# A two-layer linear-attention and Mish kernel: the last query tile's subtraction half a block sooner, low parts used later, the first block reordered

## The chip, the cores and the metric

The kernel runs on one core of a Trainium2 chip. The metric is the device time of one execution in microseconds (us); of several runs the median counts. A core has five engines with a queue of instructions each: TensorE (PE, matrix products, with weight loads listed as PEld), VectorE (DVE), ScalarE (ACT), GpSimd (POOL) and SyncE (SP, which issues the transfers from and to memory). An engine runs its own instructions in order and waits at semaphores for those of others.

## The reference

The input x has 2048 rows of 640 values; there are 32 heads of 20 values. Two layers, with the same weights, follow one another; each adds to x first the attention and then a dense part:

```python
qkv = x @ wqkv                                  # x is layer-normed
pq, pk = q @ w_phi, k @ w_phi                   # per head, 20 x 20
phi_q = concatenate([softmax(pq), softmax(-pq)])  # 40 features per head
phi_k = concatenate([softmax(pk), softmax(-pk)])
kv, z = phi_k^T v, sum over rows of phi_k
o = (phi_q kv) / (phi_q z + 1e-6)
x = x + o @ wo
h = layernorm(x) @ w1 + b1                      # 640 -> 1536
x = x + (h * tanh(softplus(h))) @ w2            # Mish
```

All of it is fp32. The two inner softmaxes need the maximum and the minimum of each head's 20 values.

## The kernel before, in words

**Precision.** A TensorE product of fp32 accuracy is made of three: each operand is split into a high part, rounded to the engine's fast fp32 format (names ending in `h`), and a low part, the remainder (`l`). A product is high x high, high x low weight, low x high weight, one matmul each; `project_half` (L399) issues these three for each of the five slices of 128 of the inner dimension. A high part is a copy by ACT, a low part a subtraction by DVE or POOL.

**Tiles and stages.** The 2048 rows are 8 blocks of 256, each of two tiles of 128. For each layer `attend_first` goes over the blocks and makes values, key features with the running sum `kv`, and query features, which go to memory; `attend_second` goes over them again: average by `kv`, divide, multiply by `wo`, add to x, and take the statistics of the next layer norm; `dense` is the Mish part.

**Folding.** w_phi is multiplied into the weights of q and k once, at the start of layer 0, so that a projection gives pq or pk (less its head's reference column) at once. `fold` (L263) is a matmul of a slice of the loaded weights (`raw`) with differences of w_phi (`big`, made by DVE at L256). A slice k of the first half (304 columns) is t = 0, 1, 2, of the second half t = 3, 4, 5, in one of five PSUM banks. `fold_parts` then makes the high part by an ACT copy (L272) and the low part by a DVE subtraction (L274): `r2h`, `r2l` for queries, `r1h`, `r1l` for keys and values.

**The first block.** For layer 0 the first block is written out by hand (L525 to L655), and for all five engines the order of the code is the order of the instructions. It holds warm-up transposes (L531, `TURNS` of them), the loads, statistics and normalization of the block's two rows of tiles, the folds, `FirstRows.turn` (L345, five transposes of a normalized tile) and `split` (high parts `xth` by ACT, low parts `xtl` by DVE, L355), the query projections of the two halves, both query tiles' features, the key folds, and the values. The value weights are not folded; `v_weights` splits them with ACT (L139) and POOL (L140) from staging tiles that SP's queue fills.

**Features** (L427): copy to SBUF by ACT (L436), maximum and minimum by DVE (L441), subtraction of the maximum (L444, by POOL for queries and DVE for keys), subtraction from the minimum (L446, DVE), exponential (ACT), sum and reciprocal (DVE, L452, L453), multiplication (POOL, L454). It is a generator: each `next` or `tail` advances it by one step.

**The second pass.** `block(b)` of `attend_second` issues for its two tiles `Rows.half(0)` and `half(1)`: 15 matmuls with `wo`, addition to x (L805) and statistics (L806). Between them stand the next block's average and the transposes of its rows (L317), their low parts `xtl` (L323), and steps of the last two query tiles' features: `tail(0)` and `tail(1)`, as many as the code says. The order of PE, SP and DVE is that of the code here. POOL also makes the low parts of the weights of the dense part (L161). The order of everything that is not said to be written out is set by the framework's list scheduler.

Of the kernel before, what the change touches and what calls it, by code (L numbers as in the profile page):

```python
# [10 lines left out]
AF = mybir.ActivationFunctionType  # L11
# [13 lines left out]
BT = 2  # L25
# [15 lines left out]
TURNS = 24  # L41
# [10 lines left out]
def kernel(  # L52
# [25 lines left out]
    def one_tile():  # L78
        return psum.tile([P, 512], F32, tag="one", name="one", bufs=4)
# [42 lines left out]
    def act(*args, **kw):  # L122

        if last_act[0] is None or written[0]:
            ins = nc.scalar.activation(*args, **kw)  # L125
        else:
            with tc.issue_after(last_act[0]):
                ins = nc.scalar.activation(*args, **kw)
        last_act[0] = ins.ins
# [5 lines left out]
    def split(hi, lo, src, stage, low=nc.vector):  # L135

        st = stage()[:, :D]
        nc.sync.dma_start(st, src)
        nc.scalar.activation(hi, st, AF.Copy)  # L139
        low.tensor_tensor(lo, st, hi.bitcast(F32), op=ALU.subtract)  # L140
# [38 lines left out]
    def v_weights(ws, low=nc.vector):  # L179

        for k in V_ORDER:
            split(ws[k][0][:, D:2 * D], ws[k][1][:, D:2 * D], wv[k * P:(k + 1) * P, :],
                  (row_tile, row_tile, v_tile, v_tile, big_tile)[k], low)
            yield
# [175 lines left out]
    def normed(b, xt):  # L360

        xn = [row_tile() for _ in range(BT)]
        for t in range(BT):
            act(xn[t], xt[:, t, :], AF.Identity,
                                 bias=stats[:, b, 1, t:t + 1], scale=stats[:, b, 0, t:t + 1])
        return Transposed(xn)
# [32 lines left out]
    def project_half(ps, xts, t, ws, col, c, ks=range(KD), w=HC, final=KD - 1):  # L399
        sl = slice(t * P, (t + 1) * P)  # L400
        cs = slice(col + c * w, col + (c + 1) * w)
        for k in ks:
            h, l, wh, wl = xts.hs[k], xts.ls[k], ws[k][0][:, cs], ws[k][1][:, cs]
            for n, (a, r) in enumerate(((h, wh), (h, wl), (l, wh))):
                nc.tensor.matmul(ps[:, :w], a[:, sl], r, start=(k == 0 and n == 0),  # L405
                                 stop=(k == final and n == 2))
# [55 lines left out]
    def attend_first(layer, x_src, first):  # L462
# [62 lines left out]
        if first is None:  # L525
            E = mybir.EngineType
            with tc.manual_schedule(engines={E.PE, E.SP, E.Activation, E.DVE, E.Pool}):
# [14 lines left out]
                def banks_of_five():  # L542
                    ma, mb = mm_tile(), mm_tile()
                    return [ma[:, 0], ma[:, 1], mb[:, 0], mb[:, 1], one_tile()]
# [18 lines left out]
                q_ws = [r2_pair(k) for k in range(KD)]  # L563
                kv_ws = [r1_pair(k) for k in range(KD)]
                xts = FirstRows()
                banks = banks_of_five()
                for t in range(2):
                    for k in range(KD):
                        fold(banks[k], bd, raw, k, t)
                turned, last = one_tile(), one_tile()  # L570
                xts.turn(0, rows[0], turned, last[:, :P])
                for k in range(KD):
                    fold(banks[k], bd, raw, k, 2)
                xts.split(0)
                query_parts(banks, 0, (0, 1))
                query_parts(banks, 0, (2, 3))
                query_parts(banks, 0, (4,))
# [3 lines left out]
                project_half(pq[0], xts, 0, q_ws, 0, 0, w=FC)  # L581
                vw = v_weights(kv_ws, nc.gpsimd)
                for _ in range(3):
                    next(vw)
                banks = banks_of_five()
                for k in range(KD):
                    for t in range(3, 6):
                        fold(banks[k], bd, raw, k, t)
                query_parts(banks, 1, (0, 1))
                normalize_first(1)  # L590
                query_parts(banks, 1, (2, 3))
                query_parts(banks, 1, (4,))
                xts.turn(1, rows[1], one_tile(), last[:, P:2 * P])
                xts.split(1)
                pq.append(one_tile())
                project_half(pq[1], xts, 0, q_ws, 0, 1, w=FC)
                next(vw)
                next(vw)
                raw = load_raw(1)
                g0 = queries(xts, 0, pq)  # L600
                next(g0)
                next(g0)
                p1 = project(xts, 1, q_ws, 0, w=FC)
                next(g0)
                g1 = queries(xts, 1, p1)
                next(g1)

# [8 lines left out]
                parts[0](0)  # L616
                next(g1)
                parts[1](0)
                parts[0](1)
                next(g1)  # L620
                parts[1](1)
                parts[2](0)
                parts[3](0)
                next(g0)
                parts[2](1)
                parts[3](1)
                parts.append(fold_keys(4))
                parts[4](0)
                vs = [v_tile() for _ in range(BT)]
                xt = fetch(x_src, 1)  # L630
                mvs = [norm_stats(t, xt) for t in range(BT)]
                norm_scale(1, mvs)
                ready = last_scale[0]
                v = [values(xts, t, vs[t]) for t in range(BT)]
                next(v[0])
                next(g1)
                parts[4](1)
                nxt = normed(1, xt)
# [114 lines left out]
    def attend_second(x_src, x_dst, acc, fetches, makes, fetch_next, begin_next):  # L753
# [41 lines left out]
        class Rows:  # L795


            def __init__(self, b, t, cur):
                self.t, self.xt, self.cur = t, xs[b], cur
                self.bn = work.tile([P, 2, 6], F32, tag="bn", name="bn", bufs=2)  # L800

            def half(self, c, ps):
                project_half(ps, self.cur, self.t, o_ws, 0, c)
                part = self.xt[:, self.t, c * HC:(c + 1) * HC]
                nc.vector.tensor_tensor(part, ps[:, :HC], part, op=ALU.add)  # L805
                nc.vector.bn_stats(self.bn[:, c], part)  # L806
# [6 lines left out]
        def block(b, cur, behind=()):  # L813
# [38 lines left out]
            for _ in range((0, 2, 1, 2)[b] if b < 4 else 0):  # L852
                tail(1)
# [254 lines left out]
```

## Time and profile before

| | us |
|---|---|
| median of 3 runs | 1361.92 |
| lowest, highest run | 1361.70, 1361.93 |
| profiled execution, its own time | 1361.4 |
| its span | 1359.6 |
| PE busy | 1348.8 (99%) |
| DVE, ACT, POOL busy | 1067.7, 585.1, 473.6 |

A row of the timeline has start, duration, engine, line, operation, output from inputs, and shape, and in brackets the idle time before it with what ended it. Matmuls overlap: a matmul's duration is longer than the step from one to the next, so that steps are read from start to start. In a list of waits stand total, count and mean.

### The profile page before, as it was taken

Reading aid. Unit: us, or ns where it says so; the run is one execution under the profiler, and the core shown is the slowest. Engines: PE = TensorE matmul, PEld = TensorE weight load, DVE = VectorE, ACT = ScalarE, POOL = GpSimd, SP = SyncE. Lnnn points to the kernel's source line nnn. Section 1 sums busy time; section 2 is a strip of 40 time slices with the busy share of each in tenths; the row PEclk is TensorE's granted clock in tenths of the full one; section 3 lists DMA queues with packets and bytes.
Section 4 is the critical chain, followed back from the end, with each engine's and each line's share of the span. In section 5 each row is a group of like instructions: output and inputs, shape, how many; then the busy total and the mean of one; then the engine's idle time right before and its main releaser. Section 6 shows DMA issues by size and latency. Waiting matters only on the chain.

```text
span 1359.6 us, 30929 instructions
## 1 busy us (share of the span) xinstructions
PE 1348.8 (99%) x12890; PEld 1335.9 (98%) x12890; DVE 1067.7 (79%) x1805; ACT 585.1 (43%) x1039; POOL 473.6 (35%) x361
## 2 busy tenths in 40 slices
PE   8999999999999999999999999999999999999998
PEld 8999999999999999999999999999999999999998
DVE  5988788887787887778778988888768776676775
ACT  5443444222454545445444344432236444444443
POOL 3345544434222222222226556743441211111111
PEclk9999999999999999999999999999999999999999
DMA  9614335798614442334473534468964231233200
GB/s 345 174 42 78 80 60 125 186 281 280 194 39 98 117 117 69 61 104 104 143 236 60 120 74 78 80 164 242 278 235 126 78 87 23 86 97 98 73 25 20
DMA packets 350613, 169.21 MB, mean 124 GB/s; under 512 B 287225, under 2 KB 323817, under 8 KB 350473
## 3 DMA queue, kind: packets, MB, share of 16 engines
q1 hardware_dynamic: 350473, 167.23, 46.0%
q8 instruction: 101, 1.65, 0.5%
q14 instruction: 39, 0.32, 0.1%
HBM read 104.61 MB, written 62.59 MB: 123 GB/s over the span
## 4 chain that ended last, share of the span: by engine, by line
PE 96%; DVE 2%; DMA 1%; ACT 0%; issue 0%; POOL 0%; SPq 0%; DVEq 0%
PE mm L405 28%; PE mm L946 25%; PE one L904 25%; PE one L405 12%; PE mm L771 3%; PE one L317 2%; PE one L490 2%; DMA big<-in_wv 0%; DVE big L446 0%; DMA raw<-in_wqk_t 0%; DVE xt L805 0%; DVE bn L806 0%; DVE r L452 0%; ACT r L125 0%; POOL r L444 0%
## 5 line engine op out<-in xcount | busy, mean ns | idle before, releaser
L946 PE MATMUL mm<-r2h,ol 128*128 128x320 f32 x1280 | 304.9, 309 | 0.0
L930 POOL TENSOR_TENSOR ol<-big,ol 128x512 fp32r<-128x512 f32 (+1 forms) x98 | 131.0, 1337 | 484.0 <-ACT ol L929 384.2
L904 PE MATMUL one<-xtl,r1h 128*128 128x256 f32 x960 | 268.2, 279 | 0.0
L904 PE MATMUL one<-xth,r1l 128*128 128x256 f32 x960 | 268.0, 279 | 0.0
L904 PE MATMUL one<-xth,r1h 128*128 128x256 f32 x960 | 265.9, 279 | 0.0
L946 PEld LDWEIGHTS mm<-r2h,ol 128*128 128x128 f32 x1280 | 219.2, 188 | 0.0
L946 PE MATMUL mm<-r2l,ol 128*128 128x320 f32 x640 | 197.3, 309 | 0.0
L405 PE MATMUL mm<-r1h,xth 128*128 128x304 f32 (+1 forms) x600 | 184.9, 308 | 0.0
L405 PE MATMUL mm<-r1l,xth 128*128 128x304 f32 (+1 forms) x600 | 183.7, 306 | 0.0
L405 PE MATMUL mm<-r1h,xtl 128*128 128x304 f32 (+1 forms) x600 | 183.5, 306 | 0.0
L904 PEld LDWEIGHTS one<-xtl,r1h 128*128 128x128 f32 x960 | 180.4, 188 | 0.0
L904 PEld LDWEIGHTS one<-xth,r1l 128*128 128x128 f32 x960 | 180.4, 188 | 0.0
L904 PEld LDWEIGHTS one<-xth,r1h 128*128 128x128 f32 x960 | 179.6, 188 | 0.0
L919 DVE TENSOR_SCALAR big<-big 128x512 f32<-128x512 f32 (+1 forms) x98 | 55.9, 571 | 113.2 <-ACT big L917 110.8
L454 POOL TENSOR_TENSOR big<-big,r 128x1280 f32<-128x1280 f32 x42 | 101.0, 2410 | 67.0 <-DVE r L453 42.8
L917 ACT ACTIVATE big<-one,b1s 128x256 f32<-128x256 f32 x192 | 80.9, 468 | 93.7 <-PE one L904 92.9
L946 PEld LDWEIGHTS mm<-r2l,ol 128*128 128x128 f32 x640 | 120.2, 188 | 0.0
L921 ACT ACTIVATE big<-big,two 128x512 f32<-128x512 f32 (+1 forms) x98 | 70.1, 716 | 113.6 <-DVE big L920 113.5
L929 ACT ACTIVATE ol<-big 128x512 fp32r<-128x512 f32 (+1 forms) x98 | 60.9, 622 | 132.9 <-DVE big L928 132.8
L405 PE MATMUL one<-r2h,xth 128*128 128x320 f32 (+1 forms) x350 | 111.5, 318 | 2.9 <-DVE xt L805 1.9
L405 PEld LDWEIGHTS mm<-r1h,xth 128*128 128x128 f32 x600 | 112.8, 188 | 0.6
L405 PEld LDWEIGHTS mm<-r1h,xtl 128*128 128x128 f32 x600 | 112.7, 188 | 0.3
(169 smaller groups left out, 3123.3 us busy)
## 6 DMA issues: line engine op xcount, KB each, us to landing
big<-e_d SPq DMA_DIRECT2D x30, 640.0 KB, 6.0
x_d<-xt SPq DMA_DIRECT2D x23, 640.0 KB, 3.9
e_d<-r SPq DMA_DIRECT2D x88, 160.0 KB, 4.1
xt<-x_d SPq DMA_DIRECT2D x22, 640.0 KB, 5.7
n_d<-xn SPq DMA_DIRECT2D x176, 80.0 KB, 2.3
xt<-in_x SPq DMA_DIRECT2D x15, 640.0 KB, 4.5
xn<-x_d SPq DMA_DIRECT2D x28, 320.0 KB, 4.3
v<-n_d SPq DMA_DIRECT2D x30, 256.0 KB, 3.2
```

What stands on the lines that cost most here:

```text
L317: nc.tensor.transpose(ps[:, c, t * P:(t + 1) * P], self.rows[t][:, (c0 + c) * P:(c0 + c + 1) * P], ident)
L405: nc.tensor.matmul(ps[:, :w], a[:, sl], r, start=(k == 0 and n == 0), stop=(k == final and n == 2))
L454: nc.gpsimd.tensor_tensor(eg, eg, r.unsqueeze(2).to_broadcast([P, 2 * H, DH]), op=ALU.mult)
L490: nc.tensor.matmul(kva[32 * q:32 * q + DH + 1, c:c + 2 * DH], v[:, (DH + 1) * h:(DH + 1) * (h + 1)], e[:, 2 * DH * h:2 * DH * (h + 1)], st ...
L771: nc.tensor.matmul(po[c][64 * q:64 * q + 64, GW * j:GW * j + w], phs[g][:n, s0:s0 + 64], kvb[:n, g, :w], start=True, stop=True)
L904: nc.tensor.matmul(ph[:, j, :], l, r, start=(n == 0), stop=(n == 3 * KD - 1))
L917: exps[0] = nc.scalar.activation(part(ta, 0)[:, j - js.start], ph[:, j, :], AF.Exp, bias=b1s[:, 2 * pr + j:2 * pr + j + 1]).ins
L919: nc.vector.tensor_scalar_min(e, e, E_CAP)
L921: nc.scalar.activation(r, n, AF.Ln, bias=two)
L929: nc.scalar.activation(ah[:, js], n, AF.Copy)
L930: nc.gpsimd.tensor_tensor(al[:, js], n, ah[:, js].bitcast(F32), op=ALU.subtract)
L946: nc.tensor.matmul(pys[t][:, c, :HC], l[:, j, sl], r, start=(f == 0 and n == 0), stop=(f == KF - 1 and n == 2))
```

## The change

The change has ten parts.

1. The warm-up has 20 transposes instead of 24.
2. In SP's queue the last three slices of the first weights stand ahead of the first block's second tile; the value weights are all loaded together next, and the key weights sooner.
3. The first tile of rows is normalized in two halves, one by ACT and one by DVE.
4. The bank order of the folds starts with another bank, and the turn of the first tile stands ahead of the last three folds of t = 1 and those of t = 2. DVE makes the differences for t = 3 to 5 later.
5. Of each half of the query weights all high parts are made first, then all low ones; the projection takes the ten products with high weights first and the five with low ones behind them. In the first half the folds of the next bank stand between.
6. ACT's order: the first value weight's copy ahead and the others behind the second tile's normalization, and the second query tile's copy ahead of the first one's exponential.
7. `pool_sub` is given as `i >= BT`: for the first two query tiles of each layer both subtractions are DVE's.
8. In the first block, the next block's statistics and normalization, and the key weights' parts, stand sooner.
9. In the first half of block 0 of the second pass the products of two slices with low inputs stand behind the four others of both.
10. In block 1 of the second pass one `tail(1)` stands ahead of the second tile's first half instead of at the block's end.

On PE, in layer 0's first block, from the warm-up to the first projections (`raw` a slice of weights, `r2h` and `r2l` high and low folded query weights, `xth` and `xtl` high and low rows). Before:

```order
L263 MATMUL mm<-big,raw_146 128x114 x4
L263 MATMUL one<-big,raw_146 128x114
L345 MATMUL one<-ident,xn 128x128 x5
L263 MATMUL mm<-big,raw_148 128x114 x4
L263 MATMUL one<-big,raw_148 128x114
L405 MATMUL one<-r2h_176,xth 128x304
L405 MATMUL one<-r2l_177,xth 128x304
L405 MATMUL one<-r2h_176,xtl 128x304
L405 MATMUL one<-r2h_178,xth 128x304
L405 MATMUL one<-r2l_179,xth 128x304
L405 MATMUL one<-r2h_178,xtl 128x304
```

And now:

```order
L273 MATMUL mm<-big,raw_142 128x114
L355 MATMUL one<-ident,xn 128x128 x5
L273 MATMUL mm<-big,raw_142 128x114 x3
L273 MATMUL one<-big,raw_144 128x114
L273 MATMUL mm<-big,raw_144 128x114 x4
L417 MATMUL one<-r2h_156,xth 128x304
L417 MATMUL one<-r2h_156,xtl 128x304
L417 MATMUL one<-r2h_158,xth 128x304
L417 MATMUL one<-r2h_158,xtl 128x304
L417 MATMUL one<-r2h_160,xth 128x304
L417 MATMUL one<-r2h_160,xtl 128x304
```

The transposes stand eight folds ahead of the first projection instead of five, and low weights come into it ten matmuls later.

On DVE, in the second pass of layer 0, block 1 (`big` the last query tile, `xt` the rows with the residual, `xtl` low parts of the next block's). Before:

```order
L810 BN_AGGR mv<-bn 128x2
L295 TENSOR_SCALAR stats<-mv,stats 128x1 x2
L805 TENSOR_TENSOR xt<-one,xt 128x320
L806 BN_STATS bn<-xt 128x6
L323 TENSOR_TENSOR xtl<-one,xth 128x512 x2
L323 TENSOR_TENSOR xtl<-one,xth 128x256
L805 TENSOR_TENSOR xt<-one,xt 128x320
L806 BN_STATS bn<-xt 128x6
L810 BN_AGGR mv<-bn 128x2
L446 TENSOR_TENSOR big<-m,big 128x32x20
L786 TENSOR_SCALAR den<-mm 128x24
```

And now:

```order
L846 BN_AGGR mv<-bn 128x2
L305 TENSOR_SCALAR stats<-mv,stats 128x1 x2
L458 TENSOR_TENSOR big<-m,big 128x32x20
L841 TENSOR_TENSOR xt<-one,xt 128x320
L842 BN_STATS bn<-xt 128x6
L333 TENSOR_TENSOR xtl<-one,xth 128x512 x2
L333 TENSOR_TENSOR xtl<-one,xth 128x256
```

The subtraction stands ahead of the second tile's first addition and of three low parts, and no longer behind them.

On POOL, in layer 1's first pass, which the list scheduler orders (`xtl` low parts of rows, `r_...` and `big` query and key tiles). Before:

```order
L323 TENSOR_TENSOR xtl<-xn,xth 128x512 x2
L454 TENSOR_TENSOR big<-big,r 128x1280
L323 TENSOR_TENSOR xtl<-xn,xth 128x256
L444 TENSOR_TENSOR big<-big,m 128x32x20
L454 TENSOR_TENSOR big<-big,r 128x1280
```

And now:

```order
L333 TENSOR_TENSOR xtl<-xn,xth 128x512
L466 TENSOR_TENSOR big<-big,r 128x1280
L333 TENSOR_TENSOR xtl<-xn,xth 128x512
L466 TENSOR_TENSOR big<-big,r 128x1280
L333 TENSOR_TENSOR xtl<-xn,xth 128x256
L456 TENSOR_TENSOR big<-big,m 128x32x20
```

A multiplication has come between the two larger low parts, so that two stand ahead of the small one instead of one.

The diff, cut to its core:

```diff
-TURNS = 24
+TURNS = 20
...
-    def project_half(ps, xts, t, ws, col, c, ks=range(KD), w=HC, final=KD - 1):
+    def project_half(ps, xts, t, ws, col, c, ks=range(KD), w=HC, final=KD - 1, ns=(0, 1, 2), end=2):
...
-            for n, (a, r) in enumerate(((h, wh), (h, wl), (l, wh))):
+            for n in ns:
+                a, r = ((h, wh), (h, wl), (l, wh))[n]
...
-            yield from features(project(xts, i % BT, q_ws, 0, w=FC) if ps is None else ps, e, True, i >= NT - 2)
+            yield from features(project(xts, i % BT, q_ws, 0, w=FC) if ps is None else ps, e, i >= BT, i >= NT - 2)
...
+                raw += load_raw(0, range(3, 6))
                 fetch_first(1)
-                raw += load_raw(0, range(3, 6))
...
+                vw = v_weights(kv_ws, nc.gpsimd, ahead=True)
...
-                normalize_first(0)
+                act(rows[0][:, :HC], xt[:, 0, :HC], AF.Identity, bias=stats[:, 0, 1, :1], scale=stats[:, 0, 0, :1])
+                nc.vector.tensor_scalar(rows[0][:, HC:], xt[:, 0, HC:], stats[:, 0, 0, :1], stats[:, 0, 1, :1],
+                                        op0=ALU.mult, op1=ALU.add)
...
+                query_folds(0, range(KD))
+                query_folds(1, range(2))
+                turned, last = one_tile(), one_tile()
+                xts.turn(0, rows[0], turned, last[:, :P])
+                xts.split(0)
+                query_folds(1, range(2, KD))
+                query_folds(2, range(KD))
...
+                query_high(*range(KD))
+                query_low(*range(KD))
+                raw_k = load_raw(1)
...
+                project_half(pq[0], xts, 0, q_ws, 0, 0, w=FC, ns=(0, 2), end=None)
+                next(vw)
+                banks = banks_of_five()
+                for t in range(3, 6):
+                    fold(banks[0], bd, raw, 0, t)
+                query_parts(banks, 1, (0,))
+                project_half(pq[0], xts, 0, q_ws, 0, 0, w=FC, ns=(1,), end=1)
+                for k in range(1, KD):
+                    for t in range(3, 6):
+                        fold(banks[k], bd, raw, k, t)
+                normalize_first(1)
+                query_parts(banks, 1, (1, 2))
+                query_parts(banks, 1, (3, 4))
...
             def half(self, c, ps):
-                project_half(ps, self.cur, self.t, o_ws, 0, c)
+                if self.b == self.t == c == 0:
+                    for ks in ((0, 1), (2, 3), (4,)):
+                        for ns in ((0, 1), (2,)):
+                            project_half(ps, self.cur, 0, o_ws, 0, 0, ks, ns=ns)
+                else:
+                    project_half(ps, self.cur, self.t, o_ws, 0, c)
...
+            if b == 1:
+                tail(1)
             if b == NB - 2:
...
-            for _ in range((0, 2, 1, 2)[b] if b < 4 else 0):
+            for _ in range((0, 1, 1, 2)[b] if b < 4 else 0):
```

More of the change, by code (lines that the diff above doesn't have):

```diff
@@ L358, in row_tile, with normed_rows @@
         return work.tile([P, D], F32, tag="xn", name="xn", bufs=4)
+    def normed_rows(b, xt):
+        xn = [row_tile() for _ in range(BT)]
+        normalize(b, xn, [xt[:, t, :] for t in range(BT)])
+        return xn
     def normed(b, xt):
[L362 to L366, printed above, removed]
+        return Transposed(normed_rows(b, xt))
     def normalize(b, dst, src):
@@ L631, in attend_first @@
                 mvs = [norm_stats(t, xt) for t in range(BT)]
+                for k in range(2):
+                    for n in range(2):
+                        parts[k](n)
                 norm_scale(1, mvs)
                 ready = last_scale[0]
+                next(g1)
+                parts[2](0)
+                parts[3](0)
+                parts[2](1)
+                parts[3](1)
+                nxt_rows = normed_rows(1, xt)
+                next(g1)
+                next(g0)
+                parts.append(fold_keys(4))
+                parts[4](0)
+                parts[4](1)
                 v = [values(xts, t, vs[t]) for t in range(BT)]
```

96 lines of the change are left out of this document (39 added, 57 removed).

## The prediction

> **What bounds the kernel now.** I read the page's busy shares and chain first, then the waits of TensorE, then the windows, and last the timelines of the places where TensorE waits.
>
> ```profile
> span 1359.6 us, 30929 instructions
> PE 1348.8 (99%) x12890; PEld 1335.9 (98%) x12890; DVE 1067.7 (79%) x1805; ACT 585.1 (43%) x1039; POOL 473.6 (35%) x361
> PE 96%; DVE 2%; DMA 1%; ACT 0%; issue 0%; POOL 0%; SPq 0%; DVEq 0%
> ```
>
> TensorE (PE) is busy for 1348.8 of 1359.6 us and carries 96% of the chain that ended last. The matmuls are, in kind and number, the same after the change but for four warm-up transposes, so only time that PE loses between them can be won. The waits of PE, grouped (total, count, mean of one), and two windows (length; busy PE, weight loads, DVE, ACT, POOL; granted clock, DMA share, GB/s):
>
> ```profile
> PE one L405 <- DVE xt L805: 1.9, 2, 0.9
> PE one L405 <- DVE r2l L274: 1.4, 2, 1.0
> PE one L405 <- DVE xtl L323: 0.3, 2, 0.2
> 0.00:42.00 42.00, 38.48 (x281) 36.95 (x282) 25.23 (x61) 22.11 (x50) 15.90 (x21) 1.00 0.97 346
> 42.00:255.00 213.00, 213.00 (x2570) 210.23 (x2570) 179.68 (x259) 91.74 (x157) 101.91 (x65) 1.00 0.43 89
> ```
>
> Three groups hold 3.6 us: a residual addition that PE waits for once per layer, low weight parts at the start, and a low part at the start of each second pass. The first 42 us lack 3.5 us of PE work; the 213 us behind them lack none, and DVE, busy for 180 of those, still delays nobody. Idle times count the modelled end of the last matmul, so below I use start against start.
>
> **The change, part by part: the start.** PE there:
>
> ```profile
> 1.34 4.38 PE L531 MATMUL one<-ident 128*128 128x128 f32 x24 [1.34 <-POOL ident masks.py:199]
> 5.87 1.12 PE L263 MATMUL mm<-big,raw 120*128 120x114 f32 x8 [0.15 <-DMA raw<-in_wqk_t]
> 8.54 0.71 PE L345 MATMUL one<-ident,xn 128*128 128x128 f32 x5
> 10.41 0.40 PE L405 MATMUL one<-r2h,xth 128*128 128x304 f32 x1
> 11.31 0.41 PE L405 MATMUL one<-r2l,xth 128*128 128x304 f32 x1 [0.49 <-DVE r2l L274]
> 11.55 0.30 PE L405 MATMUL one<-r2h,xtl 128*128 128x304 f32 x1
> 11.69 0.30 PE L405 MATMUL one<-r2h,xth 128*128 128x304 f32 x1
> 17.00 0.76 PE L345 MATMUL one<-ident,xn 128*128 128x128 f32 x5
> 18.71 0.41 PE L405 MATMUL one<-r2h,xth 128*128 128x304 f32 x1 [0.95 <-DVE r2l L274]
> 30.82 1.31 PE L263 MATMUL mm<-big,raw 120*128 120x114 f32 x10 [0.23 <-DVE r1l L274]
> ```
>
> The first fold at 5.87 waits for its weights from memory, and their loads stay where they are in the queue; so the four warm-up transposes fewer gain nothing, and I cost them at zero, covered by that load. A matmul takes 0.14 (11.55 to 11.69). From 10.41 to 11.31 one matmul stands, so 0.76 is lost; from 17.00 to 18.71 stand five transposes (0.11 each, 0.55 in all), so 1.16 is lost; the wait at 30.82 is worth 0.2 to 0.4. The engines that feed these places:
>
> ```profile
> 14.94 0.21 DVE L295 TENSOR_SCALAR stats<-mv,stats 128x1 f32<-128x1 f32 x1 [0.96 <-POOL stats L291]
> 9.18 0.83 ACT L125 ACTIVATE xth<-one 128x256 fp32r<-128x256 f32 x3 [1.79 <-PE one L345]
> 9.88 1.52 ACT L272 ACTIVATE r2h<-mm 128x342 fp32r<-128x342 f32 x4
> 16.02 0.92 ACT L125 ACTIVATE xn<-xt,stats 128x640 f32<-128x640 f32 x1
> ```
>
> In the first half, the first turn goes ahead of eight folds: two on ACT and DVE at once instead of ACT alone (0.92 for a row) make the normalized row sooner, and the ten matmuls with high weights stand ahead of the five with low ones, with three folds of the next part between. So the wait at 11.31 (0.76) goes; ACT's five copies of high parts (four in 1.52, 0.38 each, so 1.9) may pace the ten matmuls (1.4), so up to 0.5 of it comes back as slower steps. I give this half no price of its own, because what follows it is paced by the second half's turn.
>
> The second half decides. Its turn at 17.00 follows the normalization, ACT 16.02 to 16.94, which stands behind copies of folded and of value weights although the statistics it needs were there at 15.15 (14.94 + 0.21). With the copies behind it, it starts at 15.1 and ends at about 16.0. The first matmul then comes as soon after the turn as the high part allows: 8.54 to 9.18 for the first turned tiles, plus 0.28 for the first of three copies, is 0.92. So the first matmul of that half stands at 16.9 instead of 18.71, 16.6 if the copy is quicker; and the folds ahead of it, twelve of two matmuls each, end at 15.9 by my count, so nothing of them is in the way. Gain 1.8 to 2.1. With the 0.2 to 0.4 at 30.82, whose low parts now all stand before the values, it is 2.0 to 2.5.
>
> Against it: two query tiles do both subtractions of their minima on DVE instead of one on POOL. In before they read (DVE, POOL; POOL's low parts; and what DVE has to do behind them):
>
> ```profile
> 24.00 0.82 DVE L446 TENSOR_TENSOR r<-m,r 128x640 f32<-128x640 f32 x1 [0.72 <-POOL r L444]
> 19.39 3.11 POOL L140 TENSOR_TENSOR r1l<-v,r1h 128x640 fp32r<-128x640 f32 x2
> 34.04 0.84 DVE L274 TENSOR_TENSOR r1l<-one,r1h 128x342 fp32r<-128x342 f32 x2
> ```
>
> Two more of 0.82 on DVE put the last low part of the keys 1.6 later against a PE that comes 2 sooner. The second tile's values take the bank from which that part is read. The first tile's values begin 1.3 to 1.5 behind 30.82, less 2.4, so at 29.9, and their 30 matmuls at 0.147 (the step of such matmuls without a wait) take 4.4: the second tile's come at 34.3. DVE's part ended at 34.88; 2.1 sooner and 1.6 later it ends at 34.4: next to no wait, or, when a subtraction stands behind a POOL instruction of 1.55, one of up to 0.9. I take 0.4: a sum for the start of −1.8, between −1.2 and −2.3.
>
> **The second pass.** Layer 0, blocks 0 and 1:
>
> ```profile
> 257.21 0.30 PE L405 MATMUL one<-r2l,xth 128*128 128x320 f32 x1
> 257.68 0.42 PE L405 MATMUL one<-r2h,xtl 128*128 128x320 f32 x1 [0.17 <-DVE xtl L323]
> 277.08 0.49 DVE L805 TENSOR_TENSOR xt<-one,xt 128x320 f32<-128x320 f32 x1 [0.19 <-PE one L405]
> 276.88 1.25 PE L317 MATMUL one<-ident,xn 128*128 128x128 f32 x10
> 277.89 0.40 PE L405 MATMUL one<-r2h,xth 128*128 128x320 f32 x1
> 280.33 3.48 POOL L161 TENSOR_TENSOR r1l<-raw,r1h 128x1536 fp32r<-128x1536 f32 x1 [3.36 <-ACT r1h L128]
> 281.55 2.93 DVE L446 TENSOR_TENSOR big<-m,big 128x640 f32<-128x640 f32 x1
> 289.67 1.51 PE L317 MATMUL one<-ident,xn 128*128 128x128 f32 x10
> 292.10 0.41 PE L405 MATMUL one<-r2h,xth 128*128 128x320 f32 x1 [0.93 <-DVE xt L805]
> L446 DVE TENSOR_TENSOR big<-m,big x42: 759/816/2978, 53.2 to 943.2; 128x640 f32<-128x640 f32 x42
> ```
>
> The last query tile's subtraction at 281.55 takes 2.93, against a median of 0.82 for its line, because POOL subtracts low weight parts from 280.33 to 283.81: it ends 0.67 behind that. DVE is then 2.1 late, its additions slide, and at 292.10 PE waits. From ten transposes to the next matmul it is 1.0 at 276.88 and 2.43 here, of which I count 1.3 as lost (the transposes themselves took 0.26 longer, and some of that may be modelled); in each layer, since the group of waits has two. Now the subtraction stands ahead of the addition that is at 277.08, where POOL is idle for 3.36 before 280.33: 0.82. The addition moves to about 277.5, and the next matmul to 278.05, 0.16 later; that is 0 if the subtraction starts at 276.8, 0.5 if it waits a short POOL instruction out. DVE is then 2.9 ahead at 284 and the wait at 292 has its cover. What is late next is the exponential behind it, which stays at the end of the block and then finds its input ready. Twice 1.3 − 0.2 is **−2.2**, between −1.6 and −2.4.
>
> The new order of low parts in the first half of block 0 gives the part at 257.68 two matmuls more: 0.47 from 257.21 against 0.15, so 0.3 in each layer, less what modelled ends blur: **−0.55**, between −0.3 and −0.65.
>
> **Layer 1's first pass.** Its first two query tiles change as well. POOL and PE there:
>
> ```profile
> 733.92 5.67 POOL L454 TENSOR_TENSOR r<-r,r 128x1280 f32<-128x1280 f32 x2 [10.00 <-DVE r L453]
> 739.55 2.55 POOL L323 TENSOR_TENSOR xtl<-xn,xth 128x512 fp32r<-128x512 f32 x2
> 742.08 2.38 POOL L454 TENSOR_TENSOR big<-big,r 128x1280 f32<-128x1280 f32 x1
> 744.41 0.74 POOL L323 TENSOR_TENSOR xtl<-xn,xth 128x256 fp32r<-128x256 f32 x1
> 748.00 0.30 PE L405 MATMUL mm<-r1h,xtl 128*128 128x304 f32 x1
> ```
>
> The order of after puts one more multiplication (2.38) ahead of the last low part. That part is ready at 745.15 and used at 748.00: 2.85 in hand, less 2.38, less what two more subtractions on DVE (1.6) make the multiplications late, is a wait of 1.1; two subtractions less on POOL (2.6) take it away again. I take +0.6, between 0 and 2.
>
> [...]
>
> The sum: −1.8 − 2.2 − 0.55 + 0.6 = −3.95. The profiled execution had a span of 1359.6 and a time of 1361.4, so it comes to 1357.45; the median of the runs, 1361.92, stands 0.5 above it, so **1358.0**.
>
> **The rivals.** [...]
>
> *The wait only moves*: the subtraction ahead of the addition delays PE at 277.89 by as much as it won at 292.10, so the change gives −1.8 − 0.55 + 0.6 = −1.75, or 1360.2. Against it: only 0.82 with POOL idle, and 0.3 of cover.
>
> *A colder start*: 24 transposes took 4.38, 0.18 each against 0.11 for later ones, so the first ran slower; if after 20 of them PE is still slow when the folds start, their first ten matmuls (eight in 1.12) take about 1.0 more: 1359.0. [...]
>
> *Slower*: in layer 1 both extra subtractions fall behind POOL instructions (2.98 each by line L446's largest), the low parts behind the multiplications again (2.38), and the next block repeats it: 2 x 2.98 + 2.38 − 2.85 = 5.5, and 2.38 more in the block behind, 7.9, is 1361.92 − 4.55 + 7.9 = 1365.3. It decides from 7.3 us of new waits. Against it: in the like stretch of layer 0 (42 to 255) PE waits for nothing with DVE busy for 84% of it (179.68 of 213), and the groups of PE's waits name none there.
>
> **How the numbers follow.** 0.2% (2.7 us) is about what a measurement of this kernel can tell from no change: faster lies under 1359.2, slower over 1364.6. My forecast has 0.60, with 1356.4 to 1359.2 as its own range (the terms' better ends, −2.3 − 2.4 − 0.65 + 0, give −5.35 and 1356.6; a little more for the runs); the cold start 0.05; shared waits 0.16; the moved wait 0.08; slower 0.11. Half the cold start counts as faster. So faster 0.62, same 0.27, slower 0.11. The range goes from 1356.4 to 1361.8: it holds the first four cases and leaves out 0.11 above and some 0.07 below and between.
>
> **What would show it.** In the profile after: PE's group on the addition gone (right), or a new one at the same line with half a block's distance (the wait moved); the turn of the second half near 16.0 and the following matmul near 16.9; the first key fold 2 us sooner than 25; the last subtraction of the second pass 0.82 long and at about 277 less the gain of the start. Wrong would be: waits of PE in layer 1 at about 745 for a low part made by POOL, PE waiting at about 34 for a low part of the keys, or the first folds taking twice 1.12.

## The result and the profile after

The changed kernel takes 1357.78 us in the median of 6 runs (1356.74 to 1358.86), the kernel before 1362.12 in 6 runs beside it (1361.70 to 1363.51). The ratio is 0.9966 with a 95% interval of 0.9953 to 0.9979: 4.3 us less. The forecast was 1358.0. A second set of 5 runs gave 1357.64 (ratio 0.9964, 0.9951 to 0.9978).

One thing has to be known before the traces are compared: the profiled execution of the changed kernel was the slowest of its first six, 1358.86. It shows only 2.5 of the 4.3 us, and the rest is in its first 10 us, as will be seen. The second set left another profiled execution (1356.91), and both are used here.

The page of the changed kernel, first profiled execution, and its waits of PE (total, count, mean):

```profile
span 1357.0 us, 30926 instructions
PE 1349.5 (99%) x12886; PEld 1337.6 (99%) x12886; DVE 1069.5 (79%) x1810; ACT 584.5 (43%) x1039; POOL 469.3 (35%) x357
PE one L273 <- DMA raw<-in_wqk_t: 0.6, 1, 0.6
PE mm L802 <- issue: 0.6, 1, 0.6
PE one L417 <- DVE r1l L284: 0.4, 1, 0.4
```

The two waits of 0.9 for the residual addition are gone, so are those for low query weights and for the low part of block 0; there is a new one for a low part of the key weights, and the first weights came 0.6 late.

**The second pass.** DVE and PE in block 1 of layer 0, of the changed kernel:

```profile
276.41 0.81 DVE L458 TENSOR_TENSOR big<-m,big 128x640 f32<-128x640 f32 x1
277.14 0.48 DVE L841 TENSOR_TENSOR xt<-one,xt 128x320 f32<-128x320 f32 x1
276.49 1.25 PE L327 MATMUL one<-ident,xn 128*128 128x128 f32 x10
277.68 0.42 PE L417 MATMUL one<-r2h,xth 128*128 128x320 f32 x1
289.48 1.25 PE L327 MATMUL one<-ident,xn 128*128 128x128 f32 x10
290.49 0.40 PE L417 MATMUL one<-r2h,xth 128*128 128x320 f32 x1
```

The subtraction takes 0.81 where it took 2.93. The matmul behind the first transposes comes 1.19 after them, it was 1.01: 0.2 lost, since the addition moved. Behind the next transposes it comes 1.01 after them where it was 2.43: 1.4 won.

**The start.** PE in the first execution, and below it in the second one:

```profile
1.34 4.53 PE L543 MATMUL one<-ident 128*128 128x128 f32 x20 [1.34 <-POOL ident masks.py:199]
6.50 0.75 PE L273 MATMUL one<-big,raw 120*128 120x114 f32 x2 [0.63 <-DMA raw<-in_wqk_t]
7.04 1.92 PE L273 MATMUL mm<-big,raw 120*128 120x114 f32 x8
10.44 0.82 PE L273 MATMUL mm<-big,raw 120*128 120x114 f32 x6
18.06 0.77 PE L355 MATMUL one<-ident,xn 128*128 128x128 f32 x5
18.58 0.39 PE L417 MATMUL one<-r2h,xth 128*128 128x304 f32 x1
36.66 0.42 PE L417 MATMUL one<-r1h,xth 128*128 128x320 f32 x1 [0.43 <-DVE r1l L284]
```

```profile
6.14 0.74 PE L273 MATMUL one<-big,raw 120*128 120x114 f32 x2 [0.27 <-DMA raw<-in_wqk_t]
6.68 1.40 PE L273 MATMUL mm<-big,raw 120*128 120x114 f32 x8
8.91 0.82 PE L273 MATMUL mm<-big,raw 120*128 120x114 f32 x6
16.54 0.77 PE L355 MATMUL one<-ident,xn 128*128 128x128 f32 x5
17.06 0.39 PE L417 MATMUL one<-r2h,xth 128*128 128x304 f32 x1
35.15 0.42 PE L417 MATMUL one<-r1h,xth 128*128 128x320 f32 x1 [0.44 <-DVE r1l L284]
```

In the first execution eight folding matmuls take 1.92 against 1.12 before, the second turn comes at 18.06, later than the 17.00 of before, and the values' second tile at 36.66, where before it was as late. In the second execution the turn is at 16.54 and everything behind it 1.5 sooner. Both stand only 0.52 from the turn to the next matmul, where before it was 1.71.

To follow where time goes, I took for each trace the start of the same matmul, counted from the last one (the order is the same but for a few places), and subtracted it from its start in the profiled execution of before. Differences of that number between two places are what was won (positive) or lost between them:

| us won against before | start, to 60 | second pass, layer 0, 254 to 300 | 690 to 745 | 745 to 760 | 914 to 930 | 930 to 956 |
|---|---|---|---|---|---|---|
| after, first | 0.11 | 1.53 | −0.09 | −0.33 | 0.12 | 1.24 |
| after, second | 1.62 | 1.51 | −0.45 | −0.31 | 0.92 | 1.23 |

The last four columns belong to layer 1: the way into its first pass, its first pass, the start of its second pass, and block 1 of that. Between these places nothing moves by more than 0.1. Two columns, 690 to 745 and 914 to 930, differ from execution to execution, also where nothing was changed (below). The rest of the table is the change: about 1.6 at the start, 1.5 in each second pass, −0.3 in layer 1's first pass.

### The profile page after: what moved, and what is told of

Same layout as the page of the kernel before. It is cut to its first block, busy times and chain, and to the rows that moved or that the text cites. A ratio compares the mean times of both kernels' runs of the same rounds, so it can differ in the third digit from the quotient of the medians.

```text
span 1357.0 us, 30926 instructions
## 1 busy us (share of the span) xinstructions
PE 1349.5 (99%) x12886; PEld 1337.6 (99%) x12886; DVE 1069.5 (79%) x1810; ACT 584.5 (43%) x1039; POOL 469.3 (35%) x357
## 3 DMA queue, kind: packets, MB, share of 16 engines
q8 instruction: 101, 1.65, 0.5%
## 4 chain that ended last, share of the span: by engine, by line
PE 98%; DVE 1%; DMA 0%; ACT 0%; issue 0%; SPq 0%; DVEq 0%; ACTq 0%
PE mm L417 28%; PE mm L984 25%; PE one L942 25%; PE one L417 13%; PE mm L802 3%; PE one L327 2%; PE one L502 2%; PE mm L273 0%; DMA raw<-in_wqk_t 0%; DVE r1l L284 0%; PE one L802 0%; DVE m L453 0%; DVE r L458 0%; DVE r L456 0%; PE one L273 0%
## 5 line engine op out<-in xcount | busy, mean ns | idle before, releaser
L417 PEld LDWEIGHTS mm<-r1l,xth 128*128 128x128 f32 x600 | 113.0, 188 | 0.0
```

## The experiments

Four kernels that take the change apart, first.

**The subtraction alone.** Edit of the kernel before:

```diff
+            if b == 1:
+                tail(1)
             if b == NB - 2:
...
-            for _ in range((0, 2, 1, 2)[b] if b < 4 else 0):
+            for _ in range((0, 1, 1, 2)[b] if b < 4 else 0):
```

> The kernel before with part 10 alone: the last query tile's subtraction in block 1 of the second pass stands ahead of the second tile's first half. Theory (the subtraction falls out of POOL's low part, and PE's wait of 0.93 for the addition goes in both layers): 2.2 to 2.6 us less than before, and no PE wait for the addition in the trace. Rival (the wait only moves to the addition just behind the subtraction): within 0.3 us of before, with two new waits of about 0.9 half a block sooner.

Measured: 1360.11 (11 runs) against 1362.38, ratio 0.9982 (0.9973 to 0.9991): 2.3 less. In the trace 0.0 is won at the start, 1.22 in layer 0's second pass, 1.24 in layer 1's. The waits of PE there:

```profile
PE one L405 <- DVE r2l L274: 1.4, 2, 0.9
PE one L531 <- POOL ident masks.py:199: 1.3, 1, 1.3
PE mm L771 <- issue: 0.6, 1, 0.6
PE mm L263 <- DVE r1l L274: 0.4, 1, 0.4
PE one L405 <- DVE xtl L323: 0.3, 2, 0.2
```

No wait for the addition is left and none took its place. The rival, a wait that only moves, falls: 0.2 of 1.4 moved.

**The start alone** (the changed kernel without parts 9 and 10).

```diff
             def half(self, c, ps):
-                if self.b == self.t == c == 0:
-                    for ks in ((0, 1), (2, 3), (4,)):
-                        for ns in ((0, 1), (2,)):
-                            project_half(ps, self.cur, 0, o_ws, 0, 0, ks, ns=ns)
-                else:
-                    project_half(ps, self.cur, self.t, o_ws, 0, c)
+                project_half(ps, self.cur, self.t, o_ws, 0, c)
...
-            if b == 1:
-                tail(1)
...
-            for _ in range((0, 1, 1, 2)[b] if b < 4 else 0):
+            for _ in range((0, 2, 1, 2)[b] if b < 4 else 0):
```

> The kernel after without parts 9 and 10, so the new start and the subtractions on DVE alone. Theory A (the start is really won, and the profiled execution of after hides it by a late first weight and slow matmuls): 1.2 to 2.0 us less than before in the median, and in a profile without the slow matmuls the first rows of block 1 are turned about 1.5 us sooner than 41.04. Theory B (the start wins nothing, as the profiled execution of after shows): between 0.2 less and 0.5 more.

Measured: 1360.62 (11 runs), ratio 0.9987 (0.9978 to 0.9996): 1.8 less. Its trace, with first folds at 5.66, wins 2.09 up to 60 and loses 0.31 between 745 and 760. Theory A holds: the start is won, and the first profiled execution of the changed kernel hides it. With parts 9 and 10 the two make 1.8 + 2.3 + 0.6 (0.29 in each layer's trace for part 9) = 4.7, against 4.3 to 4.6 measured.

**Warm-up transposes**, 24 in the changed kernel and 20 in the one before.

```diff
-TURNS = 20
+TURNS = 24
```

> The kernel after with 24 warm-up transposes instead of 20. Theory (with 20, PE stands idle ahead of the first folds and these then run at half their rate; 24 reach up to the folds): the first folds run at 0.11 a matmul, and the median is 0.5 to 1.5 us below that of after. Rival (the rate changes by a clock that has nothing to do with the number of transposes): same median as after within 0.3 us, and slow folds as often.

> The kernel before with 20 warm-up transposes instead of 24. Theory (fewer transposes leave the first folds slow): 0.5 to 1.5 us more than before, with folds of 0.21 a matmul in the profile. Rival (no part in it): the same within 0.3 us. By the prediction's term for the transposes: zero.

Measured: the changed kernel with 24 gave 1357.16 (5 runs; ratio 0.9964, 0.9951 to 0.9977), the kernel before with 20 gave 1362.30 (11 runs; ratio 1.0002, 0.9993 to 1.0011). The second is no change, as the prediction had it, and the first is not to be told from the changed kernel. In the trace with 24 the transposes reach up to the first fold at 6.52 and the folds run at 0.11 a matmul from 6.92. I ran both once more side by side:

> The kernel after unchanged, for a second look at its start. Theory (its profiled execution was one with a late first weight and slow folds): if the first fold starts before about 6, rows of block 1 are turned 1.5 to 2.1 us sooner than in before; if it starts after 6.3 with the folds at half rate, about as in before. The median 1357.8 as found.

> The kernel after with 24 transposes once more, beside after itself. Theory (24 reach up to late first weights): the folds run at full rate from the third or fourth, and the median is 0.4 to 1 us below that of after. Rival: the same median within 0.3 us.

Measured: 1357.64 and 1357.98, 5 runs each (ratio of the second 0.9962, 0.9950 to 0.9975). My theory that 24 would bring 0.4 to 1 us falls: the number of transposes does not matter in the median. In the second look at the start the first fold came at 6.14, between the two cases that I had named, and 1.62 was won, as in the first of them.

**What the DVE subtractions of part 7 are worth.** First in both layers, then in layer 1 alone:

```diff
-            yield from features(project(xts, i % BT, q_ws, 0, w=FC) if ps is None else ps, e, i >= BT, i >= NT - 2)
+            yield from features(project(xts, i % BT, q_ws, 0, w=FC) if ps is None else ps, e, True, i >= NT - 2)
```

> The kernel after without part 7: POOL takes the subtraction of the maximum from the first two query tiles again, in both layers. Theory (DVE, with both subtractions held up by POOL's low parts, delays the keys' last low part, on which PE waits at 36.7 for 0.43; and layer 1's first pass loses 0.3 for the multiplication ahead of the low part): the wait at 36.7 and the loss of 0.3 at 753 go, 0.5 to 0.9 us less than after. Rival (the subtraction on POOL delays the value weights' low parts by as much): another wait at the values, and the same time as after within 0.3 us.

Measured: 1359.51 (11 runs), ratio 0.9980 (0.9971 to 0.9988), so 1.7 more than the changed kernel's 1357.78 and 1.9 more than its second set's 1357.64, where I had expected 0.5 to 0.9 less. In the trace 0.66 is lost at the start where the others win 1.6. POOL, DVE and PE there:

```profile
21.97 3.06 POOL L144 TENSOR_TENSOR r1l<-v,r1h 128x640 fp32r<-128x640 f32 x2
24.98 1.27 POOL L456 TENSOR_TENSOR r<-r,m 128x640 f32<-128x640 f32 x1
26.29 0.82 DVE L458 TENSOR_TENSOR r<-m,r 128x640 f32<-128x640 f32 x1 [4.95 <-POOL r L456]
29.13 0.86 DVE L284 TENSOR_TENSOR r1l<-mm,r1h 128x342 fp32r<-128x342 f32 x2
30.14 1.59 PE L273 MATMUL mm<-big,raw 120*128 120x114 f32 x9 [1.47 <-DVE r1l L284]
```

POOL's subtraction has to wait for the value weights' low parts until 24.98; DVE stands idle for 4.95 until it is done and can then make its own subtraction, the low key weights come behind that, and the last key fold waits for their bank. The rival named POOL's queue rightly but the wrong victim: not the value weights, the key folds. Of the 2.3 between −0.66 and 1.62, the wait is 1.5, less the 0.6 of the wait at the values, which this kernel does not have; the rest, some 1.4, is a stretch of slow matmuls behind the wait (granted clock 0.66 from 30 to 35, last section). That it is not this one execution alone, the 1.7 to 1.9 of the medians say. In the changed kernel both subtractions are done on DVE in that time (the rows are of the first execution, DVE then POOL):

```profile
23.04 1.43 DVE L456 TENSOR_TENSOR r<-r,m 128x640 f32<-128x640 f32 x1
24.50 2.06 DVE L458 TENSOR_TENSOR r<-m,r 128x640 f32<-128x640 f32 x1
23.74 4.23 POOL L144 TENSOR_TENSOR r1l<-v,r1h 128x640 fp32r<-128x640 f32 x2
```

Beside each other both take longer: 3.49 for two subtractions with medians of 0.82, and 4.23 for the two low parts on POOL, which took 3.11 before. That is still cheaper than the queue.

```diff
-            yield from features(project(xts, i % BT, q_ws, 0, w=FC) if ps is None else ps, e, i >= BT, i >= NT - 2)
+            yield from features(project(xts, i % BT, q_ws, 0, w=FC) if ps is None else ps, e, layer or i >= BT, i >= NT - 2)
```

> The kernel after with part 7 undone in layer 1 only. Theory (the other order of POOL costs PE 0.3 in layer 1's first pass): between the stages at 720 and at 780 nothing is lost against before, 0.3 us less than after, which the times alone may not tell. The term of the prediction: 0.6 less. Rival: nothing moves there, and the 0.3 is an effect of something else.

> The kernel after with 24 warm-up transposes and part 7 undone in layer 1 only. Theory (each of the two gives its part): 1356.5 to 1357.2, 0.5 to 1.2 us below after and 5 to 6 below before; the first folds at full rate in the profile even where the first weights are late. Rival (neither matters in the median): 1357.8.

Measured: 1356.85 (5 runs; ratio 0.9965, 0.9953 to 0.9978), and with 24 transposes 1356.42 (5 runs; ratio 0.9960, 0.9947 to 0.9972). In both traces nothing is lost between 745 and 760, as in all kernels without part 7 in layer 1, and 0.31 to 0.33 is lost there in all five traces with it. What makes it is not POOL's low part: no wait of PE stands there. It is the order of PE, which the list scheduler makes. In the first execution of the changed kernel, and then in the run with part 7 undone in layer 1:

```profile
746.31 0.30 PE L417 MATMUL mm<-r1l,xth 128*128 128x304 f32 x1
746.54 0.27 PE L502 MATMUL one<-big,v 128*21 128x40 f32 x6
746.74 0.41 PE L417 MATMUL mm<-r1h,xtl 128*128 128x304 f32 x1
746.98 0.30 PE L417 MATMUL mm<-r1h,xth 128*128 128x304 f32 x1
...
749.17 1.41 PE L502 MATMUL one<-big,v 128*21 128x40 f32 x122
```

```profile
748.82 1.48 PE L502 MATMUL one<-big,v 128*21 128x40 f32 x128
```

The small matmuls that add to `kv`, 128 in one piece, are split into 6 and 122, and two steps around the 6 are longer (746.31 to 746.54 and 746.74 to 746.98 are 0.23 and 0.24, where the step is 0.14). The two longer steps account for 0.19 of the 0.3. By the times alone the runs of 1356.85 and 1356.42, the lowest medians of all here, cannot be told from the changed kernel; both are faster than before. Five runs do not settle whether the two parts add up (1356.5 to 1357.2 expected) or neither matters (1357.8).

**Why the subtraction took 2.93.** The kernel before, with the subtraction where it was, and without a low part that POOL makes beside it. My first edit left out the wrong one:

```diff
-                    make_parts((w1s if kind == "w1" else w2s)[n], raws.pop(n), True)
+                    if kind == "w1" and n == 0:
+                        for st, cs in raws.pop(n):
+                            act(w1s[0][0][:, cs], st, AF.Copy)
+                            act(w1s[0][1][:, cs], st, AF.Copy)
+                    else:
+                        make_parts((w1s if kind == "w1" else w2s)[n], raws.pop(n), True)
```

> The kernel before, which leaves out POOL's subtraction for the low part of the first 128 rows of w1 in both layers (a copy by ACT of the weights stands in its place, so that part of the dense product is wrong); the last query tile's subtraction stays where it was. Theory (that subtraction takes 2.93 only because POOL reads at the same time, and the wait of PE at 292 comes from these 2.1): it takes 0.82, the two waits of 0.93 go, and the time is 2.4 to 2.9 us less than before. Rival (the subtraction's place behind the addition makes the wait): the waits stay, same time as before within 0.3 us.

Measured: 1362.68 (11 runs), ratio 1.0002 (0.9993 to 1.0011), subtraction 2.93, both waits of 0.9 there. The low part of the first rows is made one block sooner, and the one at 280 is that of the second rows. So this run became a control: one such instruction less on POOL elsewhere changes nothing. The same edit with `n == 1`:

> The kernel before, which leaves out POOL's subtraction for the low part of the second 128 rows of w1 in both layers (an ACT copy of the weights stands in its place, so that part of the dense product is wrong): the POOL instruction that runs from 280.33 to 283.81. Theory (the last query tile's subtraction takes 2.93 because of it, and PE's wait at 292 comes from these 2.1): 0.82, the two waits of 0.93 gone, 2.4 to 2.9 us less than before. Rival (the place of the subtraction makes the wait): still 2.93 or still the waits, same time as before within 0.3 us.

Measured: 1359.73 (12 runs), ratio 0.9980 (0.9971 to 0.9988): 2.5 less. DVE and PE in that trace, whose times are 1.6 late from its first block, where the matmuls ran slowly for 3.4 us (last section):

```profile
283.17 0.77 DVE L446 TENSOR_TENSOR big<-m,big 128x640 f32<-128x640 f32 x1
291.29 1.25 PE L317 MATMUL one<-ident,xn 128*128 128x128 f32 x10
292.30 0.39 PE L405 MATMUL one<-r2h,xth 128*128 128x320 f32 x1
```

0.77 instead of 2.93, and 1.01 instead of 2.43 behind the transposes; 1.43 and 1.44 are won in the two second passes. So the wait was made by POOL's subtraction at the same time and not by the subtraction's place as such. In the rows above, of 3.49 and 4.23, working side by side gained nothing either: one after another the four instructions take 4.75 (2 x 0.82 + 3.11), and they were done in 4.93 (23.04 to 27.97). There both sides were slowed, and not only the later one.

**The new wait at the values.** The run with 24 transposes and part 7 in layer 0 alone, with this edit:

```diff
-                next(g1)
                 parts[2](0)
                 parts[3](0)
                 parts[2](1)
                 parts[3](1)
+                next(g1)
```

> The kernel of the run with 24 transposes and part 7 in layer 0 alone, with the low parts of the key weights' slices 2 and 3 ahead of the second query tile's maxima and subtractions on DVE. Theory (these subtractions hold up the low part on which PE waits for 0.5 at 36): the wait goes, 0.5 to 0.7 us less in the profile than that run. Rival (the exponential, then late, holds up the ACT copies behind it): a new wait of PE at 40 to 45 of the same size.

Measured: 1358.57 (5 runs), ratio 0.9969 (0.9957 to 0.9981), 2.1 more than without the edit. The wait at 36 went and a larger one came. ACT and PE:

```profile
36.48 1.27 ACT L125 ACTIVATE r<-r 128x1280 f32<-128x1280 f32 x1 [5.81 <-DVE r L458]
38.27 0.77 ACT L125 ACTIVATE v<-one 128x320 f32<-128x320 f32 x2
38.76 0.42 PE L417 MATMUL one<-r1h,xth 128*128 128x320 f32 x1 [2.16 <-ACT v L125]
```

The exponential waits 5.81 for the later subtractions, and the copies of the first tile's values stand behind it on ACT; PE waits 2.16 for the bank that they read; from 39 to 44 its matmuls then run at a granted clock of 0.66. The rival's mechanism is right, at 2.2 instead of the 0.6 that was to be won.

## Why the prediction was right, and where it was not

The time, 1357.78, is 0.2 from the forecast, and the sum of the terms as now measured is about 1.6 + 2.5 + 0.6 − 0.3 = 4.4 where 3.95 was forecast. Point by point:

- **The moved subtraction**, −2.2 forecast: 1.22 and 1.24 in the trace with it alone, 2.3 by the times. Cause (POOL beside it), size in the new place (0.81), the addition's shift (0.2 against the forecast 0.16) and the wait that goes (1.4 against 1.3) hold. The reading of the transposes' extra 0.26 as partly modelled was too careful: all of the 1.4 came back.
- **Block 0's low parts**, −0.55 forecast: 0.29 in each layer.
- **The start**, −1.8 forecast: 1.57 to 2.25 in six of the seven traces that have the new start unedited and part 7 in layer 0, 0.11 in the seventh, 1.8 by the times without parts 9 and 10. The size is right; the path to it was partly wrong. I had the second half's turn at 16.0 and the matmul 0.92 behind it, because the high part of the turned tile should come first. But that matmul belongs to the first tile, which was turned long before; of the weights it needs the high part of slice 0 alone. What it waited for in the row at 18.71, `r2l`, is none of its inputs: it writes the buffer of `one` from which DVE was still reading the last fold, that of slice 4. With the new bank order of part 4 this buffer holds the fold of slice 0, and DVE has read it long before (the kernel before, then the second execution):

```profile
18.23 0.42 DVE L274 TENSOR_TENSOR r2l<-one,r2h 128x266 fp32r<-128x266 f32 x1
15.39 0.43 DVE L284 TENSOR_TENSOR r2l<-one,r2h 128x266 fp32r<-128x266 f32 x1
```

So it comes 0.52 after the turn, not 0.92. What I had wrong is the cause of this wait: the bank order removes it, and to that part I gave no price. With the old order the matmul would have had to stand until the last low part is read, at 18.54 instead of 17.06 in the second execution by my estimate from its rows; no run has the bank order alone. The turn came at 15.89 to 16.54 in the six traces, 16.3 in the mean, rather than 16.0, and the matmul behind it at 16.8 in the mean, where I had 16.9. The two misses cancel, and that this term came out is in part luck.
- **Both subtractions on DVE, layer 0**, a cost of 0.4: the wait at the values is there, 0.43 by its row and 0.6 from step to step. What I did not see is that the new start cannot do without it: with POOL's subtraction back, 1.7 to 1.9 is lost by the medians (2.3 in one trace). To cost this part I compared it with a POOL that was free, and in the changed order it is not, until 25.
- **Layer 1**, +0.6: 0.3, and by another mechanism. The step "one more multiplication ahead of the last low part is a wait of 1.1" failed: no wait. The loss is the split of the small matmuls in PE's order.
- **Shared waits**, a chance of 0.16: moved subtractions that POOL's work slows, with the worse ends of two ranges, −1.2 for the start and +2 for layer 1, estimates of mine that no run shows. Slow subtractions are there, at the start (1.43 and 2.06 for the two) and in layer 1 (2.87 for one beside a multiplication of POOL, at 721.73 in the first execution). But the start did not fall to −1.2, and layer 1 cost 0.3 instead of 2.
- **Transposes**, zero: the runs with 20 and 24 show no difference. The rival of a colder start had the right mechanism for one execution and a price that was too low (1.0 forecast, 1.5 between the two executions of the changed kernel), but the number of transposes does not decide on it in the median.

The sign "first folds taking twice 1.12" that was to make the prediction wrong did come, nearly, in the first profiled execution (1.92 for 1.12). One execution's start is not the kernel's.

## What to carry to other kernels

Where a subtraction of DVE runs beside one of POOL, look for one instruction whose duration is far from the median of its line (here 2.93 against 0.82), and move it to a place where the other engine is idle: here that was 2.3 of 4.3 us for two lines of code. Before an operation is moved from one engine to another, its price is read against the queue of that engine in the new order, not the old one. Where PE waits for a low part, look whether that part is an input of its matmul or only the last reader of the bank that the matmul writes: in the second case another bank order may be enough. And one profile of a start is not enough: a wait that cost 1.2 in one execution came to 2.7 in another, with a slow stretch behind it.

## What the runs showed that was not expected

**Slow stretches behind waits of PE.** In three of the 14 traces a stretch of slow matmuls stands right behind a wait of PE in the first block, and the granted clock shows it. The windows of the run with POOL's second low part left out (length; busy PE with count, granted clock, DMA share, GB/s), and one of the run with POOL's subtraction back:

```profile
13.60:17.00 3.40, 3.13 (x29) 1.00 1.06 401
17.00:20.40 3.40, 2.38 (x12) 0.80 1.08 343
20.40:23.80 3.40, 3.40 (x20) 0.70 1.02 330
23.80:27.20 3.40, 3.40 (x28) 1.00 1.02 408
```

```profile
30.00:35.00 5.00, 4.86 (x25) 0.66 1.04 400
```

The wait ahead of the first, from the same run's timeline:

```profile
18.79 0.44 PE L405 MATMUL one<-r2h,xth 128*128 128x304 f32 x1 [0.95 <-DVE r2l L274]
```

It is the wait for `r2l` that the kernel before has at 18.71, there without a slow stretch. With the stretch behind it 1.5 more is lost: the trace is 0.1 late at 18.79 and 1.6 late at 60. So what the new start removes was 1.2 in one execution and 2.7 in another, and one profile of before could not show that. The other two are behind waits of 1.5 and 2.2; no wait of less than 0.95 has one behind it in these traces.

What decides whether it comes is open, but can be narrowed down. The clock reads 0.50 from 19.03 to 22.44 here, from 30.77 to 34.18 in the run with POOL's subtraction back and from 40.24 to 43.65 in the run of the new wait at the values: 3.41 us each, with 1.00 on both sides. The clock's changes in this run, at 5.38, 19.03 and 22.44, lie four and one of these 3.41 apart, and those in the first execution of the changed kernel, at 10.18 and 1355.04, 394 of 3.413. I count idle time in stretches of 3.41 from each trace's first change; that such stretches run on where the clock does not change is an assumption of mine. In the stretch just ahead of the three slow ones PE is idle for 1.29, 1.47 and 1.94. Here 0.34 for the normalized rows and the 0.95 fall into one stretch. In the kernel before a border at 18.19 cuts the wait, with 0.58 of idle time in the stretch ahead of it and 0.52 in the one behind, and in two other runs, the kernel before with 20 transposes and the one without POOL's first low part, 0.95 alone in one stretch had nothing behind it (PE busy 2.45 of 3.40 from 17.00 to 20.40, clock 1.00 there and behind). Idle time alone does not settle it: 1.65 in one stretch at 915, in layer 1 of the run with POOL's subtraction back, had no slow one behind it either (clock 1.00 from 910 to 960). No run here was made to vary the idle time alone.

**The slow first matmuls.** The step of a transpose or fold is 0.21 at first and 0.11 later, and the change falls between 4.5 and 7.5 us in 13 traces, at 10.2 in the first of the changed kernel, where PE had stood idle for 0.63 while still slow. The granted clock reads 1.00 there, but a trace's record of it begins only with the change (at 4.54 in before, at 10.18 in the first of the changed kernel), so this column cannot show the first slow stretch. Counted in the same stretches of 3.41, the one just ahead of the change has PE idle for at most 0.29 in all 14 traces, and the one ahead of that for at least 0.63. In the first execution of the changed kernel the 0.63 fell between 3.36 and 6.77, and one more slow stretch followed; with 24 transposes in the new start the stretch ahead of the change has no idle time. That the idle time made it last fits this but is not shown by a run of its own. In the run with part 7 undone in layer 1 PE was idle for 1.22 at the same place, already fast, and stayed so (0.11 a matmul from 6.98).

**Stalls that belong to no kernel.** In layer 1, PE loses up to 0.9 on the way into the first pass (690 to 745; where a wait is shown, for value weights copied by ACT, 0.47 at 694 in the run without parts 9 and 10), and up to 1.7 at the start of the second, where the profile names only "issue". Both occur with and without the change: the latter is 0.6 in the changed kernel, 1.2 in the kernel before with 20 transposes, none in the run with part 7 undone in layer 1. The column 914 to 930 of the table is mostly that. What makes them is open; with the slow stretches they hide what is below about 0.5 us in the times.
